# Two attentions in one static schedule: margins, output blocks and splits at the edges set anew

## The chip, the cores and the metric

The kernel runs on one core of a Trainium2 chip, as one launch. The metric is the device time of one execution in microseconds; a time stands for the median of several runs. Matmuls run on TensorE (PE). VectorE (DVE), ScalarE (ACT) and GpSimd (POOL) do the rest; SyncE (SP), ACT and POOL issue DMA transfers.

## The reference

Two attention layers with the same sizes (2048 positions, 1024 wide, 32 heads of 32), each with its own input and weights, and their outputs side by side. All is fp32.

```python
# A: each position sees 8 keys, every second one back from itself
idx = pos[:, None] - (jnp.arange(8) * 2)[None, :]
logits = jnp.where(idx >= 0, einsum("bhsd,bhswd->bhsw", q, kg) * scale, -1e9)
a = merge(einsum("bhsw,bhswd->bhsd", softmax(logits), vg)) @ wo
# B: each position sees the 256 keys up to itself
mask = (i - j >= 0) & (i - j < 256)
p = softmax(where(mask, einsum("bhqd,bhkd->bhqk", q, k) * Dh ** -0.5, -1e9))
b = merge(einsum("bhqk,bhkd->bhqd", p, v)) @ wo
return concatenate([a, b], axis=-1)
```

Here q, k and v are the three thirds of `x @ wqkv`, and kg, vg the gathered keys and values.

## The kernel before

The work is cut into 8 units of 512 positions: units 0 to 3 are layer B ("dense"), units 4 to 7 layer A ("window"; its positions are sorted into even and odd ones first, so that a key is one of the eight before it). A unit has 8 groups (u, s) of four heads. Every fp32 operand is split into a high part (cast to fp32r) and a low part (what the cast lost), and a product is made of three matmuls, high by high, high by low and low by high.

For a group of a dense unit the steps are, with the lines that the profile names:

- q and k by 2 x 24 matmuls (L614), their eviction and low part (ACT L551, DVE L555), and six copies by SP that stack the parts (`qst`, `kst`, L575; a halo by L504).
- 16 first scores (L1024), each into one of four PSUM banks `s`; DVE takes the row maximum (L1029), ACT the exponential with its sum (L1034), and then the bank is free. These are called `ones`.
- the log-sum: ACT L1047, DVE L1052 to L1055, and one matmul (L1063, the `row`) that turns it; ACT spreads it into `qst` (L1069).
- two lots of second scores (L1108), the exponential (ACT L1115), a mask by POOL (L1093) or by DVE (L1096), and the values (L1173). The result is joined and split into `ot` by ACT and DVE (L944, L949, L956, L960).

v is made by L683 in two or three parts a unit, and the output blocks of the unit before (L747, eight a unit, stored by ACT) are put between the groups. A window group has one block of scores (L820), a softmax on DVE and ACT (L838 to L859), a spread (L868, L871) and one block of values (L892).

Weights and x come by POOL's DMA queue (L181) into three buffers `raw` and are split: a cast on ACT (L232) or DVE (L235) and subtractions on DVE (L238).

The order of all this is not written out. The kernel is built by a planner that keeps a clock of its own for every engine (class `Clock`) and four lists: `gemm` (q, k, v, output, x, in a fixed order `plan`), `ones`, `twos` (second scores and values) and `aux` (rows). At each step it takes the head of the list that is ready first. What an engine gets is in the order of these steps, so one time that is set otherwise shifts the order on every engine. Tables add to the planner's times:

- `PACE[u]`, for a dense unit: by how much later a mask may end on POOL than on DVE and still go there (L1092), margins on stacking, spread, banks and values, and last the step at which the next weight is split.
- `LATE[u][s]` is added to the time at which the stacked q and k of a group count as there (L538, L563), `HOLD[u][s]` to that of its values (L874, L1164), `AHEAD[u][s]` to the step of the next split (L617).
- `O_AT[u]` says ahead of which group the output blocks of unit u - 1 stand, and `EDGES_V[u]` at which step of the last group and last part of v the weights and x blocks of the next unit are split: `x0` to `x3`, `q0` (the next unit's first weight), `k7`, `v0`, `v1`.

```python
563  done["stack"][u, s] = max(e2, h2["hi"]) + PACE[u][1] + LATE[u][s]
617  if k == PACE[u][-1] + AHEAD[u][s]:
618      st.ahead(where["qk", u, s, t], ...)
1092 if ck.ends("pool", dur_p, r) <= ck.ends("dve", dur_d, r, port=True) + PACE[u][0]:
1093     nc.gpsimd.affine_select(w, w, ...)
...
1096 nc.vector.tensor_tensor(w, w, mask..., op=ALU.min)
1164 return latest(done["v"][u, vp], ..., masked[li] + HOLD[u][s])
```

Of the kernel before, what the change touches and what calls it, by code (L numbers as in the profile page):

```python
# [31 lines left out]
CW, CP = 0.75, 0.5  # L32
SKEW = 2
ORDER = (0, 1, 2, 3, 4, 5, 6, 7)
PACE = ((0.4, 2.4, 0.1, 0.1, 0.4, -99, 4), (0.1, 1.8, 0.3, 0.1, 0.4, -99, 2), (0.1, 0.6, 0.3, 0.1, 0.0, -99, 0), (0.2, 2.4, 0.3, 0.1, 0.0, -99, 2), (6.0, 8.0, 0.5, 0.5, 1, 2), (2.0, 6.0, 1.5, 0.2, 1, 2), (4.0, 7.0, 0.5, 0.2, 1, 3), (4.0, 7.0, 0.5, 0.0, 1, 1))
V_AT = ({0: 0, 4: 1, 7: 2}, {0: 0, 3: 1, 7: 2}, {0: 0, 5: 1, 7: 2}, {0: 0, 5: 1, 7: 2}, {0: 0, 4: 1, 7: 2}, {0: 0, 6: 1, 7: 2}, {0: 0, 6: 1, 7: 2}, {0: 0, 6: 1, 7: 2})
O_AT = ({2: (0, 1), 3: (2, 3), 4: (4, 5), 5: (6, 7)}, {3: (0, 1), 4: (2, 3), 5: (4, 5), 7: (6, 7)}, {2: (0, 1), 3: (2, 3), 4: (4, 5), 5: (6, 7)}, {2: (0, 1), 3: (2, 3), 4: (4, 5), 6: (6, 7)}, {3: (0, 1), 4: (2, 3), 5: (4, 5), 6: (6, 7)}, {2: (0, 1), 3: (2, 3), 4: (4, 5), 5: (6, 7)}, {1: (0,), 2: (1,), 3: (2, 3), 4: (4,), 5: (5,), 6: (6, 7)}, {1: (0,), 2: (1, 2), 3: (3, 4), 5: (5, 6), 6: (7,)})
# [12 lines left out]
class Clock:  # L50
# [209 lines left out]
def kernel(ctx, tc, xs, wqk, wv, wo, outs, units):  # L260
# [53 lines left out]
    def edge_of(u):  # L314
# [172 lines left out]
    def latest(*ts):  # L487
        return None if any(t is None for t in ts) else max(ts)


    def qk_items(u, s):
# [54 lines left out]
        def evac(t, ps, bank):  # L546
# [7 lines left out]
            def low():  # L554
# [38 lines left out]
        for t in range(2):  # L593
# [15 lines left out]
            def run(k, t=t, h=h):  # L609
# [31 lines left out]
    def v_items(u, part):  # L641
# [149 lines left out]
    def window(u, s):  # L791
# [71 lines left out]
        def spread(half, e):  # L863
# [137 lines left out]
    def attention(u, s):  # L1001
# [333 lines left out]
```

## Time and profile before

| | |
|---|---|
| median of 3 runs | 1785.1 us (1783.95 to 1788.92) |
| profiled execution | 1786.24 us, span 1784.5 us |
| PE | 1770.5 us busy, 15210 matmuls |
| weight loads on PE | 1472.7 us |
| DVE | 1268.0 us |
| ACT | 1054.9 us |
| POOL | 365.3 us |
| granted clock of PE | 0.999 in the mean |

The span is the time from the first to the last instruction of the program. Units 0 to 3 lie at about 0 to 1000 us, units 4 to 7 behind. PE is the busiest engine in every stage; other engines matter where PE waits for them.

### The profile page before, as it was taken

The page shows a single profiled execution, that of the slowest core. Times are in us where ns is not written, and L with a number is a line of the kernel's source. Part 1 is how long each engine was busy: PE and PEld are TensorE (multiplying, and loading weights), DVE is VectorE, ACT ScalarE, POOL GpSimd, SP SyncE. Part 2 cuts the span into 40 slices and gives each one's busy share as a digit, 9 for nine tenths or more (in the row PEclk, how much of TensorE's full clock was granted, in tenths as well). Part 3 has the DMA queues.
Part 4 walks back from the last instruction along what each step waited for, and adds up shares of the span by engine and source line. Part 5 has one row for each costly group of instructions (what it writes and reads, how often), then busy time and mean ns, then how long its engine had stood idle before and what let it go on. Part 6 is the DMA issues. An engine that isn't in the chain of part 4 may idle for free.

```text
span 1784.5 us, 39512 instructions
## 1 busy us (share of the span) xinstructions
PE 1770.5 (99%) x15210; PEld 1472.7 (83%) x15210; DVE 1268.0 (71%) x2742; ACT 1054.9 (59%) x2630; POOL 365.3 (20%) x776
## 2 busy tenths in 40 slices
PE   9999999999999999999999999999999999999999
PEld 7788888888888888888888888878888888888887
DVE  5668777777777779766667486876678666857863
ACT  5677666765667666676667355554555354534552
POOL 3222322123222313222233300110001100110000
PEclk9999999999999999999999999999999999999999
DMA  6556654647455456454653344444434443543432
GB/s 207 154 154 166 174 146 145 166 134 213 129 152 165 145 156 179 136 158 119 173 159 122 126 130 131 145 132 129 139 123 136 143 136 114 156 139 128 130 104 83
DMA packets 109724, 257.52 MB, mean 144 GB/s; under 512 B 14560, under 2 KB 29920, under 8 KB 109536
## 3 DMA queue, kind: packets, MB, share of 16 engines
q0 software_dynamic: 41760, 152.06, 27.6%
q1 hardware_dynamic: 58560, 86.15, 18.1%
q10 hardware_dynamic: 9216, 16.78, 2.5%
q8 instruction: 120, 1.97, 0.4%
q14 instruction: 68, 0.56, 0.1%
HBM read 164.63 MB, written 23.07 MB: 105 GB/s over the span
## 4 chain that ended last, share of the span: by engine, by line
PE 90%; DVE 4%; ACT 3%; DMA 2%; issue 1%; POOL 0%; SPq 0%; POOLq 0%; DVEq 0%; ACTq 0%
PE g L614 31%; PE g L747 16%; PE g L683 13%; PE s L1108 6%; PE x L614 6%; PE s L1024 5%; PE o L1173 3%; PE x L747 3%; PE x L683 2%; PE s L820 1%; DVE w L238 1%; PE x L1173 1%; DMA raw<-wv 1%; PE s L892 1%; ACT wide L868 1%
## 5 line engine op out<-in xcount | busy, mean ns | idle before, releaser
L614 PE MATMUL g<-x,w 128*128 128x512 f32 x2568 | 643.1, 393 | 0.8 <-ACT x L232 0.5
L614 PEld LDWEIGHTS g<-x,w 128*128 128x128 f32 x2568 | 476.4, 189 | 90.1 <-ACT x L232 1.0
L238 DVE TENSOR_TENSOR w<-raw,w 128x512 fp32r<-128x512 f32 x514 | 336.1, 695 | 44.6 <-ACT w L232 38.1
L1029 DVE CUSTOM_DVE_ANT_0 s<-s,mask_d 128x384 f32<-128x384 f32 (+2 forms) x512 | 262.1, 554 | 100.7 <-PE s L1024 99.6
L683 PE MATMUL g<-w,x 128*128 128x256 f32 (+1 forms) x1872 | 329.6, 320 | 1.2 <-DVE w L238 0.6
L1034 ACT ACTIVATE s<-s,nm 128x384 f32<-128x384 f32 (+2 forms) x512 | 273.8, 536 | 67.3 <-DVE nm L1029 65.7
L683 PEld LDWEIGHTS g<-w,x 128*128 128x128 f32 x1872 | 276.1, 190 | 25.0 <-DVE w L238 1.7
L747 PE MATMUL g<-ot,w 128*128 128x512 f32 x1200 | 296.2, 393 | 0.0
L747 PEld LDWEIGHTS g<-ot,w 128*128 128x128 f32 x1200 | 221.8, 188 | 43.4
L1093 POOL TENSOR_SCALAR_AFFINE_SELECT pbuf<-pbuf 128x256 f32<-128x256 f32 (+1 forms) x445 | 182.6, 435 | 212.8 <-ACT pbuf L1115 202.3
L1115 ACT ACTIVATE pbuf<-s 128x512 f32<-128x512 f32 (+1 forms) x368 | 188.9, 602 | 56.3 <-PE s L1108 50.8
L235 DVE CAST w<-raw 128x1024 fp32r<-128x1024 f32 x181 | 125.9, 695 | 67.9 <-PE g L614 24.6
L181 POOL DMA_DIRECT2D raw<-wqk x126 | 68.0, 540 | 511.9 <-DVE w L238 317.7
L1024 PE MATMUL s<-kst,qst 96*128 96x384 f32 (+2 forms) x512 | 142.2, 339 | 2.8 <-ACT s L1034 2.6
L868 ACT COPY wide<-wide 32x256 f32<-32x256 f32 x256 | 103.4, 404 | 45.8 <-DVE wide L859 42.2
L1108 PE MATMUL s<-qst,kst 128*128 128x128 f32 (+2 forms) x704 | 126.4, 307 | 0.6 <-ACT pbuf L1115 0.3
L614 PE MATMUL x<-x,w 128*128 128x512 f32 x504 | 121.8, 393 | 0.0
L1108 PEld LDWEIGHTS s<-qst,kst 128*128 128x128 f32 x704 | 107.9, 189 | 16.9 <-ACT s L1034 2.3
L1024 PEld LDWEIGHTS s<-kst,qst 96*128 96x128 f32 x512 | 92.7, 189 | 24.1 <-ACT s L1034 6.6
L614 PEld LDWEIGHTS x<-x,w 128*128 128x128 f32 x504 | 93.3, 188 | 20.2
L1034 ACT ACTIVATION_READ_ACCUMULATOR s<-s,nm 128x1 f32 x512 | 105.5, 206 | 0.2
L181 POOL DMA_DIRECT2D raw<-wv x72 | 46.4, 644 | 257.8 <-DVE w L238 97.1
(111 smaller groups left out, 1930.6 us busy)
## 6 DMA issues: line engine op xcount, KB each, us to landing
raw<-wqk POOLq DMA_DIRECT2D x126, 512.0 KB, 4.0
raw<-wv POOLq DMA_DIRECT2D x72, 512.0 KB, 4.4
raw<-wo POOLq DMA_DIRECT2D x64, 512.0 KB, 3.9
qst<-nat SPq DMA_DIRECT2D x96, 256.0 KB, 4.1
kst<-nat SPq DMA_DIRECT2D x96, 256.0 KB, 5.4
raw<-xs POOLq DMA_DIRECT2D x28, 512.0 KB, 4.9
outs<-ost ACTq DMA_DIRECT2D x56, 256.0 KB, 2.6
kst<-halo SPq DMA_DIRECT2D x72, 128.0 KB, 2.8
```

Source lines behind the costliest of these rows:

```text
L235: nc.vector.tensor_copy(t[:, 0, :], raw)
L238: nc.vector.tensor_tensor(t[:, 1, c:c + 512], raw[:, c:c + 512], t[:, 0, c:c + 512].bitcast(F32), op=ALU.subtract)
L614: nc.tensor.matmul(h["ps"], h["w"][:, a, k * P:(k + 1) * P], xt[u][k][:, b, :], start=(k == 0 and i == 0), stop=(k == NK - 1 and i == 2))
L683: nc.tensor.matmul(ps, xt[u][kw * g + k][:, a, p0:p0 + P], h["w"][g][:, c, k], start=(first and t == 0 and half == 0), stop=(last and t == 2),
L747: nc.tensor.matmul(h["ps"], w[:, a, c:c + P], ot[u, k][:, b, :], start=(k == 0 and i == 0), stop=(k == NK - 1 and i == 2))
L868: nc.scalar.copy(diag[r:r + 32, :, :, c:c + 32], pieces[r:r + 32, :, :, 1 + i % 2, :])
L1024: nc.tensor.matmul(ps[:, :n], q[0:96, j, b * P:(b + 1) * P], kk[0:96, j, c0:c1], start=True, stop=True)
L1029: nc.vector.tensor_tensor_reduce(ps[:, :n], ps[:, :n], mask[:, cut:full], scale=-1.0, scalar=BIG, op0=ALU.add, op1=ALU.min, accum_out=nm)
L1034: nc.scalar.activation(ps[:, :n], ps[:, :n], AF.Exp, bias=nm, scale=-1.0, accum_out=sm)
L1093: nc.gpsimd.affine_select(w, w, pattern=[[0, m], [step, n]], compare_op=ALU.is_ge, fill=0.0, base=base, channel_multiplier=chan)
L1108: nc.tensor.matmul(ps[:, x:x + w], kk[:, j, 256 + kb * P:256 + (kb + 1) * P], q[:, j, q0:q0 + w], start=True, stop=True)
L1115: nc.scalar.activation(w, ps[:, :m * n].rearrange("p (j n) -> p j n", j=m), AF.Exp)
```

## The change

Only numbers in the tables differ. No operation is added, removed or given another shape. The lines of PACE (five of its eight entries), LATE, HOLD, AHEAD, O_AT and EDGES_V change; two of them:

```diff
-LATE = ((7, 0, 1.5, 0, 0, 0, 0, 0), (1.5, 3, 5.5, 2, 0, 0, 0, 0), (0, 1.5, 0, 0, 0.5, 3, 0, 0), (0, 0, 0, 0, 0, 0, 0, 0), ...)
+LATE = ((7, 0, 1.5, 1.5, 0, 0, 0, 0), (1.5, 3, 5.5, 2, -0.5, 0.5, 4, 4.5), (3, 1.5, 0, 4, 0.5, 3, -0.5, 4), (2, 0, 0, 0, 0, 0, 0, 0), ...)
```

In words, the others: PACE of unit 1 lets a mask end 0.4 us later on POOL instead of 0.1, that of units 2 and 3 changes the step of the next split (0 to 2, 2 to 1) and in unit 3 adds 0.4 to the cost of values; in unit 4 the step is 3 instead of 2, and in unit 7 a cast is put on DVE rather than ACT (0.5 to -0.5). HOLD gets entries for four groups of units 1 to 3 (1.2, 1.6, -0.4, 1.2), AHEAD is set anew for three. O_AT moves output blocks 6 and 7 from ahead of group 5 to ahead of group 6 in unit 2, and blocks 1, 6 and 7 in unit 3. EDGES_V moves `q0` of unit 1 from step 32 to 28; `x1` of unit 2 from 22 to 19 and `x2` from 26 to 30 (behind `q0`, 27); `x2` of unit 3 from 24 to 28; the four x blocks of unit 5 two steps forward; `x0` of unit 6 from 10 to 8 and `v0` from 10 to 11.

PE at the end of unit 1 (v by L683, then the first q of unit 2 by L614), from the fifth `one` of group (1, 6) on. Before:

```order
L1024 MATMUL s<-kst_114,qst_112 128x384 x2
L683 MATMUL g<-w,x 128x256 x12
L1024 MATMUL s<-kst_114,qst_112 128x384
L683 MATMUL g<-w,x 128x256 x6
L1024 MATMUL s<-kst_114,qst_112 128x384 x4
L614 MATMUL g<-x,w 128x512 x18
L1024 MATMUL s<-kst_114,qst_112 128x384 x2
```

The changed kernel at the same place, from the fifth `one` on:

```order
L1024 MATMUL s<-kst_114,qst_112 128x384 x2
L683 MATMUL g<-w,x 128x256 x6
L1024 MATMUL s<-kst_114,qst_112 128x384 x2
L614 MATMUL g<-x,w 128x512 x6
L1173 MATMUL o<-pbuf,vbuf_124 32x320 x4
L1173 MATMUL x<-pbuf,vbuf_124 32x320 x4
L1173 MATMUL o<-pbuf,vbuf_124 32x192 x4
L1173 MATMUL x<-pbuf,vbuf_124 32x256 x4
L1173 MATMUL o<-pbuf,vbuf_124 32x128 x4
L1173 MATMUL x<-pbuf,vbuf_124 32x64 x4
L1024 MATMUL s<-kst_114,qst_112 128x384 x2
L614 MATMUL g<-x,w 128x512 x6
```

Four `ones` in a row have become pairs, with other matmuls between them, and the values of the group before stand between the pairs.

DVE at the same place (`w` is a weight block, `x` half an x block; the `ISA` rows are the maximum and the reading of its result). Before:

```order
L949 TENSOR_TENSOR pbuf<-o,pbuf 128x512
L1029 ISA s,nm<-s,mask_d 128x384
L1029 ISA nm 128x1
L235 CAST w<-raw 128x1024
L238 TENSOR_TENSOR w<-raw,w 128x512 x2
L235 CAST x<-raw 128x512
L238 TENSOR_TENSOR x<-raw,x 128x512
L235 CAST x<-raw 128x512
L238 TENSOR_TENSOR x<-raw,x 128x512
L1029 ISA s,nm<-s,mask_d 128x384
```

And changed:

```order
L1029 ISA s,nm<-s,mask_d 128x384
L1029 ISA nm 128x1
L235 CAST x<-raw 128x512
L238 TENSOR_TENSOR x<-raw,x 128x512
L235 CAST x<-raw 128x512
L238 TENSOR_TENSOR x<-raw,x 128x512
L1029 ISA s,nm<-s,mask_d 128x384
```

The weight's split has left this place (it stands ahead of the two maxima before); the x block is still there.

DVE at the log-sum of group (1, 7), from its last maximum to the operands of its `row` (`hl`). Before:

```order
L1029 ISA s,nm<-s,mask_d 128x384
L1029 ISA nm 128x1
L235 CAST w<-raw 128x1024
L238 TENSOR_TENSOR w<-raw,w 128x512 x2
L949 TENSOR_TENSOR pbuf<-o,pbuf 128x512
L1052 TENSOR_TENSOR nl<-nm,ln 128x16
L1054 CAST hl<-nl 128x16
L1055 TENSOR_TENSOR hl<-nl,hl 128x16
```

And changed:

```order
L1029 ISA s,nm<-s,mask_d 128x384
L1029 ISA nm 128x1
L949 TENSOR_TENSOR pbuf<-o,pbuf 128x512
L960 TENSOR_TENSOR ot<-pbuf,ot 128x512
L1052 TENSOR_TENSOR nl<-nm,ln 128x16
L1054 CAST hl<-nl 128x16
L1055 TENSOR_TENSOR hl<-nl,hl 128x16
L235 CAST w<-raw 128x1024
L238 TENSOR_TENSOR w<-raw,w 128x512 x2
```

The weight's split now stands behind the operands of the `row`, and L960 ahead of them.

More of the change, by code (lines that the diff above doesn't have):

```diff
@@ L34 @@
 ORDER = (0, 1, 2, 3, 4, 5, 6, 7)
-PACE = ((0.4, 2.4, 0.1, 0.1, 0.4, -99, 4), (0.1, 1.8, 0.3, 0.1, 0.4, -99, 2), (0.1, 0.6, 0.3, 0.1, 0.0, -99, 0), (0.2, 2.4, 0.3, 0.1, 0.0, -99, 2), (6.0, 8.0, 0.5, 0.5, 1, 2), (2.0, 6.0, 1.5, 0.2, 1, 2), (4.0, 7.0, 0.5, 0.2, 1, 3), (4.0, 7.0, 0.5, 0.0, 1, 1))
+PACE = ((0.4, 2.4, 0.1, 0.1, 0.4, -99, 4), (0.4, 1.8, 0.3, 0.1, 0.4, -99, 2), (0.1, 0.6, 0.3, 0.1, 0.0, -99, 2), (0.2, 2.4, 0.3, 0.1, 0.4, -99, 1), (6.0, 8.0, 0.5, 0.5, 1, 3), (2.0, 6.0, 1.5, 0.2, 1, 2), (4.0, 7.0, 0.5, 0.2, 1, 3), (4.0, 7.0, -0.5, 0.0, 1, 1))
@@ L36 @@
 V_AT = ({0: 0, 4: 1, 7: 2}, {0: 0, 3: 1, 7: 2}, {0: 0, 5: 1, 7: 2}, {0: 0, 5: 1, 7: 2}, {0: 0, 4: 1, 7: 2}, {0: 0, 6: 1, 7: 2}, {0: 0, 6: 1, 7: 2}, {0: 0, 6: 1, 7: 2})
[L37 removed]
+O_AT = ({2: (0, 1), 3: (2, 3), 4: (4, 5), 5: (6, 7)}, {3: (0, 1), 4: (2, 3), 5: (4, 5), 7: (6, 7)}, {2: (0, 1), 3: (2, 3), 4: (4, 5), 6: (6, 7)}, {2: (0,), 3: (1, 2, 3), 4: (4, 5), 5: (6,), 7: (7,)}, {3: (0, 1), 4: (2, 3), 5: (4, 5), 6: (6, 7)}, {2: (0, 1), 3: (2, 3), 4: (4, 5), 5: (6, 7)}, {1: (0,), 2: (1,), 3: (2, 3), 4: (4,), 5: (5,), 6: (6, 7)}, {1: (0,), 2: (1, 2), 3: (3, 4), 5: (5, 6), 6: (7,)})
@@ L40 @@
 EDGES_K = (((0, 'x0'), (2, 'x1'), (5, 'q0'), (6, 'x2'), (10, 'x3'), (15, 'k0')), ((1, 'q0'), (1, 'x0'), (3, 'x1'), (7, 'x2'), (11, 'x3'), (16, 'k0')), ((0, 'x0'), (4, 'x1'), (4, 'q0'), (8, 'x2'), (12, 'x3'), (16, 'k0')), ((0, 'x0'), (2, 'x1'), (5, 'q0'), (6, 'x2'), (10, 'x3'), (15, 'k0')), ((1, 'q0'), (1, 'x0'), (3, 'x1'), (7, 'x2'), (11, 'x3'), (16, 'k0')), ((0, 'x0'), (2, 'x1'), (5, 'q0'), (6, 'x2'), (10, 'x3'), (15, 'k0')), ((0, 'x0'), (4, 'x1'), (4, 'q0'), (8, 'x2'), (12, 'x3'), (16, 'k0')), ((0, 'x0'), (2, 'x1'), (5, 'q0'), (6, 'x2'), (10, 'x3'), (15, 'k0')))
-LATE = ((7, 0, 1.5, 0, 0, 0, 0, 0), (1.5, 3, 5.5, 2, 0, 0, 0, 0), (0, 1.5, 0, 0, 0.5, 3, 0, 0), (0, 0, 0, 0, 0, 0, 0, 0), (0, 0, 0, 4, 0, 0, 0, 0), (0, 0, 0, 0, 0, 0, 0, 0), (0, 0, 0, 0, 0, 0, 0, 0), (0, 0, 0, 0, 0, 0, 0, 0))
+LATE = ((7, 0, 1.5, 1.5, 0, 0, 0, 0), (1.5, 3, 5.5, 2, -0.5, 0.5, 4, 4.5), (3, 1.5, 0, 4, 0.5, 3, -0.5, 4), (2, 0, 0, 0, 0, 0, 0, 0), (0, 0, 0, 4, 0, 0, 0, 0), (0, 0, 0, 0, 0, 0, 0, 0), (0, 0, 0, 0, 0, 0, 0, 0), (0, 0, 0, 0, 0, 0, 0, 0))
@@ L42 @@
 ROWS = ((0, 0, 0, 0, 0, 0, 0, 0), (0, 0, 0, 0, 0, 0, 0, 0), (0, 0, 0, 0, 0, 0, 0, 0), (0, 0, 0.4, 0, 0, 0, 0, 0), (0, 0, 0, 0, 0.2, 0, 0, 0), (0, 0, 0, 0, 0, 0, 0, 0), (0, 0, 0, 0, 0, 0, 0, 0), (0, 0, 0, 0, 0, 0, 0, 0))
-HOLD = ((0, 1.2, 0, 0, 0, 0, 0, 0), (0, 0, 0, 0, 0, 0, 0, 0), (0.6, 0, 0, 0, 0, 0, 0, 0), (0, 0, 0, 0, 0, 0, 0, 1.2), (0, 0, 0, 0, 0, 0, 0, 0), (0, 0, 0, 0, 0, 0, 0, 0), (-0.4, 0, 0, 0, 0, 0, 0, 0), (0, 0, 0, 0, 0, 0, 0, 0))
-AHEAD = ((0, 0, 0, 2, 0, 0, 0, 0), (0, 0, 0, 0, 0, 0, 0, 0), (1, 0, 0, 3, 0, 0, 0, 0), (0, 0, 0, 0, 3, 0, 3, 0), (0, 0, 0, 0, 0, 2, 0, 0), (0, 0, 0, 0, 0, 0, 0, 0), (2, 0, 0, 0, 0, 0, 0, 0), (0, 0, 0, 0, 0, 0, 0, 0))
+HOLD = ((0, 1.2, 0, 0, 0, 0, 0, 0), (0, 0, 0, 0, 1.2, 0, 0, 0), (0.6, 0, 1.6, 0, 0, 0, 0, -0.4), (1.2, 0, 0, 0, 0, 0, 0, 1.2), (0, 0, 0, 0, 0, 0, 0, 0), (0, 0, 0, 0, 0, 0, 0, 0), (-0.4, 0, 0, 0, 0, 0, 0, 0), (0, 0, 0, 0, 0, 0, 0, 0))
@@ L45 @@
+AHEAD = ((0, 0, 0, 2, 0, 0, 0, 0), (0, 0, 0, 0, -2, 0, 0, 0), (1, 0, 0, 3, 0, 0, 0, 1), (0, 0, 0, 0, 3, 0, 4, 0), (0, 0, 0, 0, 0, 2, 0, 0), (0, 0, 0, 0, 0, 0, 0, 0), (2, 0, 0, 0, 0, 0, 0, 0), (0, 0, 0, 0, 0, 0, 0, 0))
 EARLY, WARM = 1.0, 10
```

2 lines of the change are left out of this document (1 added, 1 removed).

## The prediction

> **What bounds the kernel now.** I read the page's head, then the busy time by stages, then who TensorE (PE) waited for, and last the timeline round each wait.
>
> ```profile
> span 1784.5 us, 39512 instructions
> PE 1770.5 (99%) x15210; PEld 1472.7 (83%) x15210; DVE 1268.0 (71%) x2742; ACT 1054.9 (59%) x2630; POOL 365.3 (20%) x776
> 300.00:1100.00 800.00, 797.13 (x6471) 668.73 (x6471) 585.91 (x1442) 526.37 (x1334) 208.88 (x433) 1.00 0.52 148
> 1100.00:1785.00 685.00, 678.09 (x6746) 562.18 (x6744) 472.04 (x723) 325.32 (x750) 68.05 (x122) 1.00 0.41 130
> PE s L1024 <- ACT s L1034: 2.1, 3, 0.9
> PE s L1063 <- DVE hl L1055: 0.6, 1, 0.6
> ```
>
> PE is busy 1770.5 of 1784.5 us, and no matmul is added or taken away. So only waits can be won, and their sum is small. The stage rows give length, then busy time of PE, its weight loads, VectorE (DVE), ScalarE (ACT) and GpSimd (POOL). Between 300 and 1100 us, where nearly all of the changed order lies, PE is idle 800.00 - 797.13 = 2.87 us; the last two rows are the waits in that stage alone. The end of a matmul is modelled, so a wait costs a little more than the idle time shows; I take each from the starts of the matmuls. At full speed a 128x512 matmul takes 10.88 / 48 = 0.227 us from start to start:
>
> ```profile
> 1636.98 10.88 PE g L614 x48
> ```
>
> **Place A, group 6 of unit 1.** These are timelines of PE and DVE (start, length, what, idle time before it), and one stage of 2 us with its granted clock (the number behind the POOL count).
>
> ```profile
> 437.80 0.51 PE L1024 MATMUL s<-kst,qst 96*128 96x384 f32 x2
> 439.21 0.44 PE L1024 MATMUL s<-kst,qst 96*128 96x384 f32 x1 [0.90 <-ACT s L1034]
> 440.29 0.69 PE L1024 MATMUL s<-kst,qst 96*128 96x384 f32 x1 [0.64 <-ACT s L1034]
> 440.78 5.64 PE L614 MATMUL g<-x,w 128*128 128x512 f32 x18
> 446.25 0.51 PE L1024 MATMUL s<-kst,qst 96*128 96x384 f32 x2
> 437.77 0.69 DVE L235 CAST w<-raw 128x1024 fp32r<-128x1024 f32 x1
> 441.83 0.56 DVE L1029 CUSTOM_DVE_ANT_0 s<-s,mask_d 128x384 f32<-128x384 f32 x1
> 441.00:443.00 2.00, 2.00 (x6) 1.52 (x6) 1.97 (x7) 0.52 (x2) 0.73 (x1) 0.50 0.87 229
> ```
>
> Four score matmuls (L1024) stand in a row. Each needs one of four PSUM banks, and a bank comes free when DVE has taken the row maximum (L1029) and ACT the exponential (L1034). DVE meanwhile splits one weight block and two halves of an x block, from 437.77 to 441.83: 4.06 us in which no maximum is taken. The four matmuls last from 437.80 to 440.78, 2.98 us; with 384 of 512 columns one needs 384 / 512 x 0.227 = 0.170, four 0.68. Loss 2.30 us. Then the clock is down to 0.50, and 18 matmuls take 446.25 - 440.78 = 5.47 instead of 18 x 0.227 = 4.09: another 1.38 us. Together 3.68 us, the largest loss behind the start.
>
> [...]
>
> **The change, part by part.** *Places of x and w splits at the edges.* At the end of unit 1 the first weight of unit 2 ('q0') is split at step 28 instead of 32, so it leaves the four-microsecond block; and the four score matmuls no longer stand together. In the changed order they stand in pairs, with three or more 128x512 matmuls (0.68 us) or six of 128x256 behind each pair, and a block of values (L1173) behind the second. What remains in front of a maximum there is one x block: two casts and two subtractions, 441.83 - 439.70 = 2.13 us by the row at 439.70 below, and behind the second pair stand 6 x 0.227 = 1.36 us and the value block. I count all of 3.68 us as gone; bounds 2.30 (the clock falls all the same) and 3.68.
>
> ```profile
> 439.70 0.42 DVE L235 CAST x<-raw 128x512 fp32r<-128x512 f32 x1
> 478.41 3.70 PE L683 MATMUL g<-w,x 128*128 128x512 f32 x15
> 482.68 0.22 PE L1063 MATMUL s<-ident,hl 128*32 128x128 f32 x1 [0.57 <-DVE hl L1055]
> 479.41 0.69 DVE L235 CAST w<-raw 128x1024 fp32r<-128x1024 f32 x1 [2.55 <-PE g L683]
> 694.72 1.59 PE L614 MATMUL g<-x,w 128*128 128x512 f32 x6
> 696.90 0.45 PE L1024 MATMUL s<-kst,qst 96*128 96x384 f32 x1 [0.59 <-ACT s L1034]
> 693.53 0.69 DVE L235 CAST w<-raw 128x1024 fp32r<-128x1024 f32 x1 [0.71 <-DMA raw<-wqk]
> ```
>
> *Place B, the log-sum of group 7 of unit 1* (L1063). DVE stood 2.55 us for a weight buffer that PE still read, split the weight from 479.41 on (the cast of 0.69 and two subtractions), and only then came to the row's operands. PE: 482.68 - 478.41 = 4.27 for 15 matmuls that need 3.40, loss 0.87. The changed DVE order has no split ahead of the row. What is late next is the pair L949 and L960, which hangs on a value block; that block now stands a score and 18 L683 matmuls ahead of the row, against 15 before, but the row has only 18 x 0.227 = 4.1 us behind its last score, where it had 21 and the value block. Bounds 0 and 0.87, taken 0.87.
>
> *Place C, end of unit 2.* The weight came late by DMA (0.71 idle on DVE), and a score matmul waited behind its split: 696.90 - 694.72 = 2.18 for 6 x 0.227 = 1.36, loss 0.82. The new table splits x block 2 behind this weight (30 behind 27) instead of before it (26), so its load is issued one block earlier, and x block 1 leaves at 19 instead of 22. Taken 0.82, bounds 0 and 0.82.
>
> *Margins (LATE, HOLD).* They push first scores and values back where the plan had them too early. Two more losses lie in such places:
>
> ```profile
> 464.52 1.17 PE L1108 MATMUL s<-qst,kst 128*128 128x128 f32 x4
> 465.53 0.86 PE L683 MATMUL g<-w,x 128*128 128x512 f32 x3
> 111.68 0.87 PE L1108 MATMUL s<-qst,kst 128*128 128x384 f32 x2
> 112.39 0.88 PE L683 MATMUL g<-w,x 128*128 128x256 f32 x6
> ```
>
> Two 128- and two 384-column matmuls take 1.01 instead of 2 x 0.057 + 2 x 0.170 = 0.45, loss 0.56; two of 384 columns take 0.71 instead of 0.34, loss 0.37. In both the changed order puts about three more matmuls of 128x512 or six of 128x256 between row and second scores, 0.5 to 0.7 us, so I count both: 0.93, bounds 0 and 0.93.
>
> *Masks.* PACE of unit 1 raises the first entry from 0.1 to 0.4: a mask goes to POOL if it ends there at most 0.4 us later. Counted in the order, unit 1 has 54 masks fewer on DVE and as many more on POOL; in the other units at most 7 change sides, either way.
>
> ```profile
> L1096 DVE TENSOR_TENSOR pbuf<-pbuf,keep_f 128x256 f32<-128x256 f32 x19 | 8.1, 436 | 2.1 <-ACT pbuf L1115 1.8
> L1093 POOL TENSOR_SCALAR_AFFINE_SELECT pbuf<-pbuf 128x256 f32<-128x256 f32 x46 | 22.3, 490 | 24.4 <-ACT pbuf L1115 23.4 <-PE g L614 0.4
> L1093 POOL TENSOR_SCALAR_AFFINE_SELECT pbuf<-pbuf 128x256 f32<-128x256 f32 x28 | 11.2, 403 | 15.1 <-ACT pbuf L1115 15.1
> PEld o L1173: 1.0, 3
> POOL raw L181 <- DVE w L238: 613.2, 144, 10.7
> ```
>
> The first two rows are unit 1 (202 to 450 us), the third unit 0 (46 to 202), where the margin is 0.4 already; the fourth, from the line's own view, says that in the whole run values waited for POOL's masks 1.0 us in 3 times. A mask costs 490 instead of 436 ns, 0.05 us later each, beside other matmuls: nothing on PE. If that cover is gone, see the slower rival.
>
> *Unit 6's edge and unit 7's casts.* At 1559 a weight's subtraction lay behind the four passes of a softmax:
>
> ```profile
> 1558.18 1.25 DVE L238 TENSOR_TENSOR w<-raw,w 128x512 fp32r<-128x512 f32 x2
> 1559.49 0.73 PE L683 MATMUL g<-w,x 128*128 128x512 f32 x2 [0.64 <-DVE w L238]
> ```
>
> The changed order still has it there, but an earlier weight is cast on DVE (0.69) where ACT took it; I take 0.4, between 0 and the idle 0.64. The other waits behind 1100 us keep their order.
>
> *New waits.* Three edges of units have their splits moved; two of the three cost 3.68 and 0.82 before, 2.25 in the mean. One chance in six for each: 3 x 2.25 / 6 = 1.1 us, an estimate; bounds 0 and 3.7.
>
> **Sum.** 3.68 + 0.87 + 0.82 + 0.93 + 0.40 = 6.70 less 1.1 = 5.6 us. The profiled execution took 1786.24 us with a span of 1784.5, so 1780.6 for such a one; the median of the three runs shown is 1785.1, 1.1 below it, so 1779.5 there.
>
> **Rivals.**
> 1. *The clock falls anyway.* If something else than the two waits of place A lowers it, 5.6 - 1.38 = 4.2 is won, so 1780.9. Against it: the fall follows the two waits within a microsecond, and the mean over the stage's 800 us is 1.00.
> 2. *A new block of splits.* At the end of unit 2 x blocks 2 and 3 now stand at steps 30 and 31, 2 x 2.13 = 4.3 us of DVE in one go, as long as the 4.06 of place A. If scores run into it as there, 3.68 comes back less the 1.1 already counted: 5.6 - 2.6 = 3.0, so 1782.1. Against it: at these rates no score of units 1 to 3 in the new order meets its bank again with less than 1.8 us of PE work between; at place A it was 1.3.
> 3. *Two more waits go.* The x blocks of the two last edges are split earlier; if that takes 1.2 us more from the waits in the last stage, 1778.3. For it: 6.91 us of PE idle there; against it: that order is nearly unchanged.
> 4. *Slower: masks late on POOL.* POOL works in order, and a load that waits for a buffer stood there 613.2 / 144 = 4.3 us in the mean. If a moved mask falls behind such a load, the values wait, and by place A a wait of 2.30 us brings the clock down: 3.68 a time. From two of the eight groups of unit 1 on the gain is gone; four give 14.7 - 5.6 = 9.1 us more, 1794.2. For it: the same mask takes 490 ns in unit 1 against 403 in unit 0. Against it: unit 0 runs on this margin with its waits at 1.0 us in all.
>
> [...]
>
> **How the numbers follow.** A measurement of this kernel tells about 0.3% from no change, 5.4 us, so the line is at 1779.7. Forecast 0.62, of which 0.40 beyond the line and 0.22 short of it (its bounds go from 4.2 to 6.7 us); rival 1 0.06, rival 2 0.09, rival 3 0.08, rival 4 0.15. Faster 0.40 + 0.08 = 0.48; within 0.22 + 0.06 + 0.09 = 0.37; slower 0.15. The range goes from rival 3 less the 1.1 by which the lowest run shown lies under the median, 1777.2, to no gain at all, 1785.1; it leaves out rival 4.
>
> **What would show it.** Right: no wait of L1024 on L1034 near 440 us and a clock of 1.00 there; no wait of L1063 on L1055; PE idle under 1.5 us between 300 and 1100; L1173 still waits about 1 us for L1093. Wrong: a wait over 1 us in that stage with a fall of the clock behind it, or L1173 waiting for L1093 in unit 1.

## The result, and the profile after

The changed kernel takes 1783.38 us in the median (22 runs, 1781.21 to 1787.34), the kernel before, measured beside it, 1785.75 us (22 runs, 1783.95 to 1788.92). The ratio is 0.9986 with an interval of 0.998 to 0.9992: 2.4 us less, 0.14%, where 5.6 us were forecast. The sign was right; less than half of the size came.

The profiled execution of the changed kernel took 1782.26 us, 3.98 less than that of before. The page's head:

```profile
span 1780.5 us, 39465 instructions
PE 1767.2 (99%) x15210; PEld 1472.1 (83%) x15210; DVE 1261.0 (71%) x2691; ACT 1049.9 (59%) x2628; POOL 374.1 (21%) x829
```

Its busy time by stages (length, then PE, its weight loads, DVE, ACT and GpSimd):

```profile
300.00:1100.00 800.00, 798.82 (x6480) 670.67 (x6479) 576.97 (x1391) 523.64 (x1327) 214.28 (x473) 1.00 0.53 149
1100.00:1781.00 681.00, 672.19 (x6721) 557.48 (x6719) 475.21 (x728) 320.97 (x749) 68.50 (x122) 1.00 0.42 130
```

And PE's waits (in total, times, longest): the only one in 300 to 1100 us, then the three longest from 1100 us on:

```profile
PE s L1024 <- ACT s L1034: 0.9, 1, 0.9
PE x L683 <- DVE w L238: 1.6, 1, 1.6
PE g L683 <- DVE w L238: 1.3, 1, 1.3
PE o L892 <- issue: 0.8, 1, 0.8
```

Between 300 and 1100 us (units 1 to 3) PE is idle 800.00 - 798.82 = 1.18 us instead of 2.87. Behind 1100 us it is the other way round: 680.5 - 672.19 = 8.3 us to the end of the span, where before had 684.5 - 678.09 = 6.4. (The prediction's 6.91 for before, 0.5 us more, counts on to 1785 us, past the end of its span at 1784.5.)

Not all of the 3.98 us between the two profiles is the change's. Nothing is moved ahead of the first log-sum's row (L1063). It stands in PE's timeline of before at

```profile
51.38 0.22 PE L1063 MATMUL s<-ident,hl 128*32 128x128 f32 x1
```

in that of the changed kernel at

```profile
49.29 0.22 PE L1063 MATMUL s<-ident,hl 128*32 128x128 f32 x1
```

and in an experiment below (e3), whose order up to here is that of before, at

```profile
49.13 0.22 PE L1063 MATMUL s<-ident,hl 128*32 128x128 f32 x1
```

The start takes up to 2.2 us more or less from one execution to the next. From that row to the end of the span, before takes 1784.5 - 51.38 = 1733.1 and the changed kernel 1780.5 - 49.29 = 1731.2: 1.9 us less, which goes with the 2.4 of the medians.

Place A in the changed kernel, PE's timeline:

```profile
437.00 0.62 PE L1024 MATMUL s<-kst,qst 96*128 96x384 f32 x2
437.46 1.55 PE L614 MATMUL g<-x,w 128*128 128x512 f32 x6
438.85 0.34 PE L1024 MATMUL s<-kst,qst 96*128 96x384 f32 x1
```

the stage with its granted clock (the number behind the count):

```profile
438.00:442.00 4.00, 4.00 (x20) 1.00 1.05 244
```

and place B, PE's timeline:

```profile
472.66 4.26 PE L683 MATMUL g<-w,x 128*128 128x512 f32 x18
476.95 0.22 PE L1063 MATMUL s<-ident,hl 128*32 128x128 f32 x1
```

At A the scores stand apart, none waits, and the clock is 1.00. At B 18 matmuls take 476.95 - 472.66 = 4.29 us where 18 x 0.227 = 4.09 are needed: 0.20 of loss is left of 0.87. Place C did not go as forecast. PE's timeline there:

```profile
693.09 0.51 PE L1024 MATMUL s<-kst,qst 96*128 96x384 f32 x2
694.51 0.44 PE L1024 MATMUL s<-kst,qst 96*128 96x384 f32 x1 [0.91 <-ACT s L1034]
```

and ACT's:

```profile
693.29 0.60 ACT L551 ACTIVATE nat<-g 128x512 fp32r<-128x512 f32 x1 [1.81 <-PE g L614]
693.79 0.55 ACT L1034 ACTIVATE s<-s,nm 128x384 f32<-128x384 f32 x1
```

and DVE's, the maximum that this exponential needs:

```profile
691.24 0.56 DVE L1029 CUSTOM_DVE_ANT_0 s<-s,mask_d 128x384 f32<-128x384 f32 x1
```

The third of three scores waits 694.51 - 693.09 - 2 x 0.170 = 1.08 us. The exponential (L1034) that has to free its bank has its maximum from about 691.9 us on, and ACT is idle from 691.5 to 693.29; yet it runs only behind the cast of a projection (L551) that stands ahead of it on ACT, and ACT sits 1.81 us in front of that cast until PE has finished the projection. It is a wait of another kind, 0.26 us longer than the one of before.

One more place grew between 300 and 1100 us, and no list of PE's waits shows it. PE's timeline in unit 3:

```profile
904.99 1.29 PE L1173 MATMUL o<-pbuf,vbuf 64*32 64x320 f32 x7
907.06 1.36 PE L1108 MATMUL s<-qst,kst 128*128 128x128 f32 x8
```

and GpSimd's and DVE's just ahead:

```profile
902.84 2.94 POOL L1093 TENSOR_SCALAR_AFFINE_SELECT pbuf<-pbuf 128x256 f32<-128x256 f32 x4 [0.76 <-ACT pbuf L1115]
903.12 0.89 DVE L235 CAST w<-raw 128x1024 fp32r<-128x1024 f32 x1
```

This block of value matmuls takes 907.06 - 904.99 = 2.07 us, where the other blocks of the unit take 1.24: 0.83 us are lost, in which its weight loads wait for GpSimd's masks. The four masks take 0.74 us each, against a mean of 0.45 for masks of this shape in the whole kernel, and the cast that DVE does beside them takes 0.89 instead of 0.69. Whether one of the two slows the other no run here shows. The loss is 0.8 us in e2, e4, e6, e7, e8 and e11 below as well, 0.5 in e12, and it is absent from before, e1, e3, e5, e9 and e10: it comes with the rows of units 2 and 3.

Behind 1100 us three places grew. PE's timeline at the first of them in before:

```profile
1365.09 0.73 PE L683 MATMUL x<-w,x 128*128 128x512 f32 x2 [1.07 <-DVE w L238]
```

PE's timeline at all three in the changed kernel:

```profile
1359.84 0.73 PE L683 MATMUL x<-w,x 128*128 128x512 f32 x2 [1.56 <-DVE w L238]
1554.57 0.73 PE L683 MATMUL g<-w,x 128*128 128x512 f32 x2 [1.29 <-DVE w L238]
1561.96 0.25 PE L892 MATMUL o<-wide,vbuf 64*32 64x72 f32 x2 [0.77 <-issue]
```

and DVE's ahead of the second:

```profile
1541.86 0.69 DVE L235 CAST w<-raw 128x1024 fp32r<-128x1024 f32 x1 [1.19 <-DMA raw<-wv]
```

The waits of 1.07 and 0.64 us for a weight's subtraction became 1.56 and 1.29, and a wait of 0.77 is new: 0.49 + 0.65 + 0.77 = 1.9 us more. At the second place the cast that the prediction counted on, now on DVE, has itself waited 1.19 us for its weight's transfer, and from there to the subtraction for which PE waits DVE has no idle time left in which to catch up.

### The profile page after: what moved, and what is told of

The parts are those of the page before. It is cut to its first block, busy times and chain, and to the rows that moved or that the text cites. A ratio compares the mean times of both kernels' runs of the same rounds, so it can differ in the third digit from the quotient of the medians.

```text
span 1780.5 us, 39465 instructions
## 1 busy us (share of the span) xinstructions
PE 1767.2 (99%) x15210; PEld 1472.1 (83%) x15210; DVE 1261.0 (71%) x2691; ACT 1049.9 (59%) x2628; POOL 374.1 (21%) x829
## 4 chain that ended last, share of the span: by engine, by line
PE 89%; DVE 3%; ACT 3%; DMA 3%; issue 1%; POOL 0%; SPq 0%; ACTq 0%; POOLq 0%; DVEq 0%
PE g L614 30%; PE g L747 16%; PE g L683 13%; PE x L614 6%; PE s L1108 6%; PE s L1024 5%; PE o L1173 3%; PE x L747 3%; PE x L683 2%; PE s L820 1%; PE x L1173 1%; DVE w L238 1%; DMA raw<-xs 1%; DMA qst<-nat 1%; PE s L892 1%
## 5 line engine op out<-in xcount | busy, mean ns | idle before, releaser
L614 PE MATMUL g<-x,w 128*128 128x512 f32 x2568 | 640.0, 392 | 0.5 <-ACT w L232 0.5
L614 PEld LDWEIGHTS g<-x,w 128*128 128x128 f32 x2568 | 475.5, 188 | 89.6 <-ACT w L232 0.9
L683 PE MATMUL g<-w,x 128*128 128x256 f32 (+1 forms) x1872 | 330.0, 319 | 1.9 <-DVE w L238 1.3
L1034 ACT ACTIVATE s<-s,nm 128x384 f32<-128x384 f32 (+2 forms) x512 | 274.1, 536 | 66.0 <-DVE nm L1029 64.7
L683 PEld LDWEIGHTS g<-w,x 128*128 128x128 f32 x1872 | 276.3, 190 | 25.6 <-DVE w L238 2.1
L1093 POOL TENSOR_SCALAR_AFFINE_SELECT pbuf<-pbuf 128x128 f32<-128x128 f32 (+1 forms) x498 | 191.3, 411 | 203.0 <-ACT pbuf L1115 184.5
L235 DVE CAST w<-raw 128x1024 fp32r<-128x1024 f32 x186 | 135.2, 727 | 67.5 <-PE g L614 22.5
L614 PE MATMUL x<-x,w 128*128 128x512 f32 x504 | 121.8, 393 | 0.0
L614 PEld LDWEIGHTS x<-x,w 128*128 128x128 f32 x504 | 93.3, 188 | 20.2
L1034 ACT ACTIVATION_READ_ACCUMULATOR s<-s,nm 128x1 f32 x512 | 105.9, 207 | 0.2
L181 POOL DMA_DIRECT2D raw<-wo x64 | 35.6, 556 | 332.1 <-DVE w L238 164.3
```

What stands on the lines that cost most here:

```text
L181: self.nc.gpsimd.dma_start(raw if len(ap.shape) == 2 else raw.rearrange("p (a b) -> p a b", a=2), ap)
L235: nc.vector.tensor_copy(t[:, 0, :], raw)
L614: nc.tensor.matmul(h["ps"], h["w"][:, a, k * P:(k + 1) * P], xt[u][k][:, b, :], start=(k == 0 and i == 0), stop=(k == NK - 1 and i == 2))
L683: nc.tensor.matmul(ps, xt[u][kw * g + k][:, a, p0:p0 + P], h["w"][g][:, c, k], start=(first and t == 0 and half == 0), stop=(last and t == 2),
L1034: nc.scalar.activation(ps[:, :n], ps[:, :n], AF.Exp, bias=nm, scale=-1.0, accum_out=sm)
L1093: nc.gpsimd.affine_select(w, w, pattern=[[0, m], [step, n]], compare_op=ALU.is_ge, fill=0.0, base=base, channel_multiplier=chan)
```

## The experiments

Each was run in five rounds beside the kernel before on the same chip; ratios are to that. "Loss" is time from start to start of PE's matmuls over what they need at full speed, 0.227 us for one of 128x512.

**e1: the first weight's new place alone.** Before, with one number changed:

```diff
-EDGES_V[1]: ... (20, 'x2'), (32, 'q0'), (33, 'x3')
+EDGES_V[1]: ... (20, 'x2'), (28, 'q0'), (33, 'x3')
```

> Before, with one number changed: the first weight of unit 2 is split at step 28 of unit 1's edge instead of 32. Theory: the two waits in the row of four scores near 440 us and the fall of the clock behind them both go, 2.30 + 1.38 = 3.7 us, so the ratio to before is 0.998 and the granted clock of the stage 441 to 443 us is 1.00; the log-sum's wait near 482 us (0.87) stays. Rival: the clock falls there for a reason of its own, so 2.3 us, ratio 0.9987, and the stage still shows less than 0.9. Second rival: the split only runs into other scores, PE stays idle over 2.5 us between 300 and 1100 us, ratio 1.000.

Measured: 1786.74 against 1785.58 us, ratio 1.001 (1.0001 to 1.0019). The waits of place A are gone, and those of place B with them, but the kernel is not faster: it is slower by an amount that the interval only just tells from nothing. PE's timeline at 488 us:

```profile
488.28 0.77 PE L1024 MATMUL s<-kst,qst 96*128 96x384 f32 x3 [2.31 <-DMA halo<-nat]
```

and PE's busy time in the stage behind it, with the granted clock behind the count:

```profile
490.00:492.00 2.00, 2.00 (x8) 0.50 0.03 10
```

The whole plan behind the moved split has shifted. The first scores of unit 2 now come before the halo of their keys has landed, wait 2.31 us, and the clock falls to 0.50 behind them. Smaller waits grow too, that of place C to 1.37 us and one at 1562 us to 1.25. The number to which the prediction booked its largest term brings nothing alone. Of the three expectations the second rival came nearest (PE idle over 2.5 us between 300 and 1100; it is 800.00 - 794.72 = 5.28), but the wait is mostly one for the halo and not for the split.

**e6: the changed kernel without that number.**

```diff
-EDGES_V[1]: ... (28, 'q0'), (33, 'x3')
+EDGES_V[1]: ... (32, 'q0'), (33, 'x3')
```

> The changed kernel, with only the first weight of unit 2 put back from step 28 to 32 of unit 1's edge. Theory: weight and x block stand in one go of 4 us on VectorE again, the four scores wait at 438 to 441 us, 2 to 2.3 us of loss, so the ratio to before is 0.9997 to 1.000. Rival: the margins of the late groups alone spread the scores, no wait over 0.5 us is left there, and the ratio stays at 0.9986.

Measured: 1785.5 against 1785.5 us, ratio 1.0 (0.9992 to 1.0009): the time that the theory gave, and not by its way. The four waiting scores of place A do not come back; the late margins alone spread them, as the rival had it. Smaller waits took their place. PE:

```profile
446.50 0.45 PE L1024 MATMUL s<-kst,qst 96*128 96x384 f32 x1 [0.36 <-ACT s L1034]
461.83 0.73 PE L683 MATMUL g<-w,x 128*128 128x512 f32 x2 [0.62 <-DVE w L238]
```

With two smaller ones between them (0.16 and 0.23 us) and others of their size, the losses add up to about 2.5 us. So neither the split's place nor the margins win anything without the other.

**e5: all five rows of unit 1, and only these.**

```diff
-PACE[1]: (0.1, 1.8, ...
+PACE[1]: (0.4, 1.8, ...
-LATE[1]: (1.5, 3, 5.5, 2, 0, 0, 0, 0)
+LATE[1]: (1.5, 3, 5.5, 2, -0.5, 0.5, 4, 4.5)
-HOLD[1][4], AHEAD[1][4]: 0, 0      EDGES_V[1]: (32, 'q0')
+HOLD[1][4], AHEAD[1][4]: 1.2, -2   EDGES_V[1]: (28, 'q0')
```

> Before, with all five rows of unit 1 changed (masks' margin, late margins, hold, ahead, and the place of the first weight at step 28), and nothing else. Theory: the weight's new place alone cost 2 us because scores of group 7 then came too early for their keys; with the new margins of the late groups that wait near 488 us is gone too, and the unit has no wait over 0.3 us between 430 and 520 us: 2.30 of place A, 0.87 of place B and 0.56 of 465 us are won, 3.7 us, ratio 0.998, and 0.9972 if the clock's fall is to be had as well. Rival: the gain needs the rows of unit 2 too, since the same steps run on into them; then waits of 1 us or more stay between 430 and 520 us and the ratio is over 0.999.

Measured: 1784.48 against 1785.5 us, ratio 0.9996 (0.9987 to 1.0005). No loss over 0.2 us is left between 430 and 482 us, places A and B included. PE's timeline:

```profile
485.55 0.77 PE L1024 MATMUL s<-kst,qst 96*128 96x384 f32 x3 [2.55 <-DMA halo<-nat]
```

the stage behind the wait with its granted clock:

```profile
486.00:488.00 2.00, 2.00 (x11) 1.00 0.49 190
```

and the issue of the halo's transfer, its size and the time to its landing:

```profile
halo<-nat SPq DMA_DIRECT2D x1, 256.0 KB, 8.3
```

The same first scores of unit 2 wait 2.55 us for a halo that is 8.3 us on its way. The rival holds: unit 1's rows need something of unit 2's. That wait is 0.24 us longer than e1's 2.31, and here the clock stays at 1.00.

**e9 and e10: unit 1's rows and the late margin that was missing.** e9 is e5 with unit 0's late row and one number of unit 2's; e10 has unit 2's whole late row.

```diff
-LATE[0]: (7, 0, 1.5, 0, ...       LATE[2]: (0, 1.5, 0, 0, 0.5, 3, 0, 0)
+LATE[0]: (7, 0, 1.5, 1.5, ...     LATE[2]: (3, 1.5, 0, 0, 0.5, 3, 0, 0)
```

> Before, with the five rows of unit 1, the late margins of unit 0, and one number more: the late margin of the first group of unit 2, 0 to 3. Unit 1's rows alone left one wait of 2.5 us at 485 us, the first scores of unit 2 on the transfer of their keys' halo. Theory: that number pushes these scores behind some 15 matmuls of 128x512 more, the wait is gone, places A and B stay gone, and the places behind keep the order of before: 1.5 us or so less than the 0.9996 of unit 1's rows alone, 2.7 with the whole wait, so a ratio of 0.998 to 0.9988, at or below the whole change's 0.9986. Rival: the plan behind shifts with it and new waits of 1 us or more show between 490 and 720 us, ratio 0.9992 or more.

> The same kernel with the whole late row of unit 2 as in the changed kernel (first group 3, fourth 4, seventh -0.5, eighth 4). Theory: the late margins of the last group of unit 2 only matter at the edge of unit 2, so the wait near 695 us lies between nothing and 1.1 us; ratio as the kernel without it, within 0.0005. Rival: without the other numbers of unit 2 they make a wait of over 1.5 us near 700 us, ratio 0.9992 or more.

Measured: e9 0.9986 (0.9977 to 0.9995), e10 0.9987 (0.9978 to 0.9996). The wait for the halo is gone, and e9 already has the whole change's gain without the other rows of units 2 to 7. That is the time that the theory of e9 gave. Of the 2.7 us that e5 lost there, a part came back 20 us later, where the output projection waits for the split of an output block on DVE (L960) and loses 1.2 us, against 0.4 in e5. PE's timeline in e9:

```profile
508.00 2.12 PE L747 MATMUL g<-ot,w 128*128 128x512 f32 x8 [0.89 <-DVE ot L960]
693.61 0.44 PE L1024 MATMUL s<-kst,qst 96*128 96x384 f32 x1 [0.70 <-ACT s L1034]
```

Place C has its wait of before, in e10 as well (0.9 us of loss); the late margins of unit 2's last groups change nothing by themselves, as the theory of e10 had it.

**e8: units 2 to 4 alone.** Before, with the rows of units 2 and 3 (PACE, LATE, HOLD, AHEAD, EDGES_V, O_AT) and the one number of unit 4.

```diff
-PACE[2][6], PACE[3][4], PACE[3][6], PACE[4][5]: 0, 0.0, 2, 2
+PACE[2][6], PACE[3][4], PACE[3][6], PACE[4][5]: 2, 0.4, 1, 3
-EDGES_V[2]: ... (22, 'x1'), (26, 'x2'), (27, 'q0')
+EDGES_V[2]: ... (19, 'x1'), (27, 'q0'), (30, 'x2')
...
```

> Before, with only the rows of units 2 and 3 and the one number of unit 4 changed. Theory: place A and place B stay as before (waits of 0.90, 0.64 and 0.57), place C's wait of 0.8 us is replaced by one of 1.1 us in the projection's cast, so these rows bring nothing: ratio 1.000, and 1.0006 with the larger waits behind 1100 us that the number of unit 4 brings. Rival: they bring the rest of the changed kernel's gain, about 1 us, ratio 0.9994. The clock behind place A: if the two waits bring it down it is 0.50 for 2 us behind them here too; in one of the two executions seen so far with these very waits it stayed at 1.00.

Measured: 1786.2 against 1785.5 us, ratio 1.0004 (0.9995 to 1.0014): no gain, as the theory had it. Place C waits 0.91 us as said; place B waits 1.27 instead of the 0.57 expected, and a score wait of 0.48 us at 454 us is new. Place A has its two waits, up to 438.2 us here. The stage behind them with its granted clock:

```profile
439.00:441.00 2.00, 2.00 (x11) 1.00 0.77 243
```

And PE's timeline at place A in e3 (below), whose order there is that of before too:

```profile
436.99 0.44 PE L1024 MATMUL s<-kst,qst 96*128 96x384 f32 x1 [0.90 <-ACT s L1034]
438.07 0.44 PE L1024 MATMUL s<-kst,qst 96*128 96x384 f32 x1 [0.64 <-ACT s L1034]
438.35 4.25 PE L614 MATMUL g<-x,w 128*128 128x512 f32 x18
442.44 0.51 PE L1024 MATMUL s<-kst,qst 96*128 96x384 f32 x2
```

In e3 stand the same waits of 0.90 and 0.64 us as in before, to the hundredth, and the 18 matmuls behind them take 442.44 - 438.35 = 4.09 us, full speed, where before took 5.47.

**e4: the edge of unit 2 put back.**

```diff
-EDGES_V[2]: ... (19, 'x1'), (27, 'q0'), (30, 'x2')
+EDGES_V[2]: ... (22, 'x1'), (26, 'x2'), (27, 'q0')
```

> The changed kernel, with the edge of unit 2 put back as before (x block 1 at step 22, x block 2 at 26, ahead of the weight at 27). Theory: in the changed kernel the score wait of 0.9 us near 694 us is not the split's: ScalarE has the cast of a projection ahead of the exponentials and stands 1.8 us in it until the projection ends. With the old edge this order changes, and the wait behind a weight that comes late (0.8 us before) returns in its place, so PE idle between 300 and 1100 us stays at 1.2 to 1.5 us and the ratio to before at 0.9986. Rival: the two blocks split in one go at steps 30 and 31 make the wait, so with the old edge no wait over 0.3 us is left there, and the ratio is 0.998.

Measured: 1783.89 against 1785.58 us, ratio 0.9993 (0.9984 to 1.0002). PE's timeline:

```profile
697.75 0.44 PE L1024 MATMUL s<-kst,qst 96*128 96x384 f32 x1 [0.61 <-ACT s L1034]
705.39 0.44 PE L1024 MATMUL s<-kst,qst 96*128 96x384 f32 x1 [0.93 <-ACT s L1034]
```

and DVE's:

```profile
693.77 0.70 DVE L235 CAST w<-raw 128x1024 fp32r<-128x1024 f32 x1 [1.68 <-DMA raw<-wqk]
```

The old wait behind the late weight is back (DVE stands 1.68 us for it), and a second one comes at 705 us. So the new edge does what the prediction said of its weight; but it pays with the wait on ACT's cast. By PE's idle time between 300 and 1100 us it is worth about a microsecond, 800.00 - 797.83 = 2.17 us here against 1.18, more than the theory's 1.2 to 1.5; the times do not tell the two kernels apart, their intervals overlap. The rival, that the two blocks split in one go make that wait, falls, since waits of 0.61 and 0.93 us stand here without them.

**e12: three matmuls more in front of that wait.** The kernel of e11 (below) with one number more:

```diff
-LATE[2][7]: 4
+LATE[2][7]: 5
```

> The kernel with the edges of units 5 and 6, unit 7's margins and unit 4's number put back, and one number more: the late margin of the last group of unit 2, 4 to 5, which puts its three scores in a row near 695 us behind 24 matmuls of 128x512 instead of 21. Theory: the third of them waits for a bank whose exponential stands on ScalarE behind the cast of a projection; the cast's end does not move, so three matmuls more (0.68 us) ahead shorten the wait of 1.06 us to about 0.4 and the ratio falls from 0.9981 to 0.9978. Rival: the cast or the exponential is late for another reason and moves along, or the scores behind meet their banks later, so the wait there stays at 0.9 us or another of 0.7 us comes between 700 and 720 us, ratio 0.9981 or more.

PE's timeline:

```profile
693.76 0.52 PE L1024 MATMUL s<-kst,qst 96*128 96x384 f32 x2
694.49 0.44 PE L1024 MATMUL s<-kst,qst 96*128 96x384 f32 x1 [0.21 <-ACT s L1034]
```

and ACT's:

```profile
693.28 0.60 ACT L551 ACTIVATE nat<-g 128x512 fp32r<-128x512 f32 x1 [1.81 <-PE g L614]
```

The cast stands where it stood (693.28 against 693.29), the scores come 0.67 us later, and the third now waits 694.49 - 693.76 - 0.34 = 0.39 instead of 1.08 us. The cause of this wait is thereby shown. The time does not tell the two apart: 1782.06 against 1785.26 us, ratio 0.9983 (0.9974 to 0.9992), where e11 has 0.9981; two losses of 0.2 and 0.3 us are new, at 765 and 882 us, and the 0.9978 expected is not reached.

**e7: unit 1's margin for masks put back.**

```diff
-PACE[1]: (0.4, 1.8, ...
+PACE[1]: (0.1, 1.8, ...
```

> The changed kernel, with only the first number of unit 1's margins put back from 0.4 to 0.1, so that some 50 masks of unit 1 go back from GpSimd to VectorE (the plan of unit 1 also shifts with them). Theory of the prediction: the masks cost and bring nothing, ratio 0.9986 as in the changed kernel, within 0.0006. Rival: VectorE without these masks is what lets the maxima come in time, so with them back a score wait of 0.5 us or more shows between 430 and 520 us and the ratio is 0.9992 or more.

Measured: 1785.34 against 1785.5 us, ratio 1.0 (0.9991 to 1.0009). The theory falls: without this number the gain is gone. The rival's signs came, a score wait over 0.5 us and a ratio over 0.9992, but not by its cause. ACT's timeline near 443 us:

```profile
442.10 0.60 ACT L551 ACTIVATE nat<-g 128x512 fp32r<-128x512 f32 x1 [2.99 <-PE g L614]
```

PE's:

```profile
443.31 1.01 PE L1024 MATMUL s<-kst,qst 96*128 96x384 f32 x2 [1.08 <-ACT s L1034]
```

and, from the view of GpSimd's mask line in the changed kernel, who waited for it:

```profile
PEld o L1173: 1.8, 4
```

The masks' own share is small: values wait 1.8 us for GpSimd's masks in the changed kernel, 2.0 in e7 and 1.0 in before, and one block of values at 420 us takes 1.87 us in e7 instead of 1.24. With the number back, the plan of the unit shifts: place B's wait is back (0.58 us), and a score wait of 1.08 us appears that is place C's again. Its maximum was ready at about 439.9 us, and the exponential stands behind a cast for which ACT sits idle 2.99 us. How much of it is VectorE's time and how much the shift of the plan stays open, since one number sets both.

**e2, e3 and e11: the last units.** e2 is the changed kernel with three rows put back, e3 is before with these three rows changed, e11 is e2 with unit 4's number put back as well.

```diff
-EDGES_V[5]: ... (11, 'x0'), (18, 'x1'), (24, 'x2'), (29, 'x3')
+EDGES_V[5]: ... (13, 'x0'), (20, 'x1'), (26, 'x2'), (31, 'x3')
-EDGES_V[6]: ... (8, 'x0'), (11, 'v0')      PACE[7][2]: -0.5
+EDGES_V[6]: ... (10, 'x0'), (10, 'v0')     PACE[7][2]: 0.5
e11 only:
-PACE[4][5]: 3
+PACE[4][5]: 2
```

> The changed kernel, with three rows put back as they were before: the places of the splits at the edges of units 5 and 6 and the margin row of unit 7. Theory: these rows made the waits for a weight's subtraction near 1360 and 1555 us longer (1.6 and 1.3 us in the changed kernel, 1.1 and 0.6 before) and added the value wait of 0.8 us near 1562; with them back, PE idle behind 1100 us falls from 8.8 to about 7 us and the ratio to before is 0.9975. Rival: the longer waits come from how the earlier units arrive there or from the one number of unit 4, so nothing changes against the changed kernel, 0.9986.

> Before, with only these three rows changed (edges of units 5 and 6, margin row of unit 7). Theory: waits of 1.6 and 1.3 us near 1365 and 1559 us and one of 0.8 us near 1566, PE idle behind 1100 us 8.8 instead of 6.9 us, ratio 1.001. Rival: as before, 6.9 us, ratio 1.000. The prediction's forecast of these rows alone was a gain of 0.4 us, 0.9998.

> The changed kernel, with the edges of units 5 and 6, the margin row of unit 7 and also the one number of unit 4 put back as before. Theory: that number too does harm (value wait of 0.3 us at 906 us, projection at 953 us, 0.2 us), so the ratio is 0.9978 against 0.9981 with the three rows alone. Rival: it was set for the end of unit 3 as the new margins leave it, and without it a score waits there, 0.5 us or more between 900 and 1000 us, ratio 0.9985 or more.

Measured: e2 0.9981 (0.9973 to 0.999), e3 0.9997 (0.9989 to 1.0006), e11 0.9981 (0.9972 to 0.999). PE's waits behind 1100 us in e2, whole list but the two of 0.4 and 0.5 us that all kernels have:

```profile
PE x L683 <- DVE w L238: 1.0, 1, 1.0
PE g L683 <- DVE w L238: 1.0, 2, 0.8
PE o L892 <- issue: 0.4, 1, 0.4
```

To the end of the span PE is idle 679.7 - 672.5 = 7.2 us behind 1100 us instead of 8.3, and the median lies 0.0005 (0.9 us) below the changed kernel's; the waits show it, the intervals of the two ratios overlap. About half of the 0.9 is the clock's: among executions with a mean clock of 1.000 (10 of e2's 11, 14 of the changed kernel's 22) the medians are 1782.24 and 1782.65 us. In e3 the same two rows read:

```profile
PE x L683 <- DVE w L238: 1.6, 1, 1.6
PE g L683 <- DVE w L238: 1.1, 2, 0.8
```

The first wait is 1.6 us as expected, the second only 0.8, and there is none near 1562: a part of the harm needs the new order in front. The time of e3 does not reach the theory's 1.001, and PE's idle time from 1100 us to the end of its span, 7.4 us, lies between the 6.4 of before and the 8.3 of the changed kernel. Unit 4's number, put back, brings nothing that can be measured, and the block of values near 906 us takes 2.06 us in e11 as well, so that number is not what costs there. e2 and e11, at 0.9981, are the best versions found, 3.2 and 3.4 us under before.

## Why the prediction was right and wrong

*Place A.* The mechanism was right: four scores in a row behind 4.06 us without a maximum, and apart from each other they do not wait. Two things in the step were not. The 1.38 us for the clock were counted as a consequence of the two waits; with the same two waits the clock fell in one profiled execution of three (before; not in e3 and e8). The mean clocks on record say how often it may be. They are 0.999 in the two profiled executions that show a fall (before and e1) and 1.000 in the other twelve. Over all executions, the kernels with place A's two waits (before, e3, e8) have 0.999 or less in 59 of 130, the kernels without them in 24 of 121 (e1, with its halo wait, stands apart with 8 of 11). So a mean under 1.000 goes with these waits more often, and is neither certain with them nor absent without; that each such mean stands for a fall is an estimate from the two profiled executions that show one, and where in the kernel it came in the unprofiled executions is not on record. It is a cost that an execution may or may not have, so 2.30 was the part to be relied on, the lower bound given. And the gain was booked to the split's new place, while e1, e6, e5 and e9 show that it takes the place, the margins of unit 1 and the late margin of unit 2's first group together. As what is late next there the prediction looked at scores and DVE; it was the halo of the next unit's keys.

*Place B* came as worked out, 0.67 of 0.87. *Margins*: no wait is left at 112 and 465 us, as forecast.

*Place C* is one of two steps that failed: 0.82 gained was forecast, 0.26 was lost. The old wait went as said (e4 brings it back), but the term looked at DVE alone. In the new order ACT had a cast in front of the exponential that did not yet have its input, and, as its trace shows, it did not run the exponential first: 1.08 instead of 0.82. Rival 2 named the place, and a wrong cause; its argument against itself, that every bank had 1.8 us of PE work before it was met again, left out ACT.

*Masks* at nothing: right for unit 1, where no value matmul (L1173) waits for a mask; wrong for unit 3, where the block near 905 us loses 0.83 us to GpSimd's masks, and for the number that moves the masks, which carries the plan of the whole unit (e7). Rival 4 did not come as it was put: L1173 waited 1.8 us in four pieces, none of them in unit 1, and no clock fell in the profiled execution, where every stage of 2 us reads 1.00. Its step from a wait of 2.30 us to a fall of the clock does not hold either: in e5 the clock stayed at 1.00 behind a wait of 2.55 us.

*Unit 6's edge* is the other step that failed. Forecast at 0.4 gained, its own place (1554 us) lost 0.65 instead. The step took the cast on DVE as lightening ACT and did not ask when that cast's weight would land. The prediction had the other waits behind 1100 us keep their order; the two at 1360 and 1562 us grew by 0.49 and 0.77 more. Together the last units lost 1.9 us by the waits, 2.3 away from the 0.4 forecast. e2's rows take back a part of it, 0.4 to 0.9 us by the medians.

*New waits*, 1.1 estimated, did not cover what came: besides place C's 0.26 there are losses of 0.26, 0.83 and 0.22 us at 704, 906 and 953 us, 1.3 together, and the last units' 1.9. By places the sum is then 2.30 + 0.67 + 0.93 - 0.26 - 1.3 - 1.9 = 0.4 us, and 1.8 where the clock had fallen in before, as in the profile shown, which gained 1.9 behind the start. The medians' 2.4 has an interval of 1.4 to 3.6 (0.0008 and 0.002 of 1785.75). It does not come from the clock alone: among executions with a mean clock of 1.000 the medians are 1784.95 us for before (60 runs) and 1782.65 for the changed kernel (14), 2.3 us apart. So about 1.9 us of the medians' gain are not found at any place in the two profiles compared, and stay open.

Of the signs named for "right" three held in units 1 to 3: no score wait near 440 with the clock at 1.00, PE idle 1.18 us in 300 to 1100, no L1063 in the list of waits there. The fourth, that L1173 still waits about 1 us for masks, did not (1.8). A sign for the last units was missing, and there the gain was given back.

## What to carry to other kernels

In a static order that one planner writes, a number is not worth what it does at its place: it shifts everything behind, and parts of a change that win together can each lose alone, so a part is tested both alone and taken out of the whole. When a wait goes, follow each engine's order through the place, that of the engine that frees the buffer too: here an exponential stood behind a cast whose input was not there, on an engine that is busy 59%. Waits under a microsecond are best compared by rows at their places, since here the start alone moved the whole by 2 us from one execution to the next.

## What the runs showed of the hardware

In these runs the clock's fall cannot be read from the length of a wait. Behind the same two waits of 0.90 and 0.64 us it fell to 0.50 in one profiled execution (before) and not in two others: in e3 the 18 matmuls behind them took 4.09 us, full speed, and in e8 the stage behind them reads 1.00. Behind a wait of 2.31 us (e1) the clock fell to 0.50, behind one of 2.55 us (e5) it stayed at 1.00. What else decides it no run here shows.
